# PE transposes for the first eight groups, a spare accumulator bank for the third MLP unit of a gap, and later w_out loads

## The chip, the core and the metric

The kernel runs on one core of a Trainium2 chip. The metric is the device time of one execution in microseconds. TensorE is called PE, its weight loads PEld, VectorE DVE, ScalarE ACT, GpSimd POOL and the DMA issuer SyncE SP. A DMA can be issued from the queue of SP, ACT or POOL.

## What is computed

```python
def _attn_ref(q, k, v, g_q, g_k):                 # q, k, v: (8, 12, 448, 64)
    def rmsnorm(x, g):
        rms = np.sqrt(np.mean(x * x, axis=-1, keepdims=True) + 1e-06)
        return x / rms * g
    q_n, k_n = (rmsnorm(q, g_q), rmsnorm(k, g_k))
    scores = (1.0 / np.sqrt(64)) * np.matmul(q_n, k_n.transpose(0, 1, 3, 2))
    attn = np.exp(scores - np.max(scores, axis=-1, keepdims=True))
    attn = attn / (np.sum(attn, axis=-1, keepdims=True) + 1e-09)
    return np.matmul(attn, v)

def _moe_ref(x, w_in, w_out, alpha):              # x: (3584, 768), w_in: (768, 2048)
    h = x @ w_in
    g = np.maximum(h, 0.0) + alpha * np.minimum(h, 0.0)
    return g @ w_out                              # w_out: (2048, 768)
```

The twelve heads of a token, side by side, are the 768 columns of x.

## The kernel before

**Groups.** A group y (0 to 23) is four heads of one batch; three groups make a batch, and there are eight batches. `load_qk` (L92) brings q and k of a group into the tile nat (six buffers, so three groups). `square`, `reduce`, `root` and `scale` (L127 to L162) make the normalised fp16 tile qs: a product on POOL, a reduction (ss) on DVE, a logarithm and an exponential of the small tile rr on ACT, and a product with rr on POOL. (For the first groups ACT or DVE does some of these products.) Then q and k must be transposed, so that the 64 channels lie on partitions: qT and kT.

**Two ways to transpose.** For groups 0, 1 and 2, `turn` (L174) issues 14 transposes on PE into PSUM and two evictions on DVE, of which the one for k also multiplies with the gains (`gain`). From group 3 on, `turn_dma` (L164) issues two DMA transposes on SP from qs to qT and kT, and `turn` is only the multiplication of kT with the gains on DVE (L178).

**Attention.** For each of the seven key tiles of a group, `score` (L207) does four matmuls into sc, and `soft` (L221) one exponential on ACT into expT. `den` and `attv` (L244, L257) are 28 matmuls each into an accumulator: dn, the sums of the exponentials, and av. Between them ACT inverts dn (`log` L248, `invert` L253), and after them DVE multiplies av with the inverse into xT (L263).

**MLP units.** An up unit (L268) is six matmuls into hT, an ACT copy (ah, L280) and a DVE maximum (gT, L281). A down unit (L285) is 16 matmuls into op and a DVE copy (osb, L301), with the output DMAs after the second half of a token tile.

**PSUM.** The pool pss holds two sc tiles of two banks, psa one accumulator tile of two banks (tag acc: dn, av, tps), psf two tiles of one bank (tag mm: hT, op, the filler matmuls of `spin`, and ct, through which alpha and the gains reach their partitions). A tile of a pool is reused in turn, and its next writer waits until its last reader is done.

**Order.** All engines work in program order, which the loop at L462 writes out by hand in 66 bursts. A burst has two or three key tiles (score and soft), then the den or the attv of an earlier group if one is due, then root and scale (and turn_dma) of a later group, then a gap: MLP units, with the `turn` of the next group behind the first of them. `prep` holds what is issued ahead of a burst (loads, squares), `post` and `jobs` what comes after it or inside a down unit (reductions). Bursts 0 to 11 have two key tiles each and no MLP units: den 0 and attv 0 are in bursts 4 and 5, den 1 and attv 1 in 7 and 8, den 2 in 11. Up to burst 11 a `spin(4)` ends each burst: four matmuls whose result nobody reads. Burst 12 (`first`) has attv 2 and the first up units. A burst without den and attv is called plain (`plain`). What comes after burst 65 is the list `rest`.

**Planner.** L388 to L410 spread the units of a batch over its bursts by fixed costs (1.13 for an up unit, 2.6 for a down unit, `cost(n)` for the rest of a burst). They decide only the order.

Of the kernel before, what the change touches and what calls it, by code (L numbers as in the profile page):

```python
# [9 lines left out]
FP32 = mybir.dt.float32  # L10
FP16 = mybir.dt.float16
# [10 lines left out]
def kernel(  # L22
# [12 lines left out]
    nc = tc.nc  # L35

    B, H, S, D = q.shape
    DM = H * D
    DF = moe_w_in.shape[1]
    J = S // 64  # L40
    HH = H // 2
    G = HH // 2
    KM = DM // 128
    NF = DF // 128
    OH = DM // 2
    W = 2 * S
    NG = B * G
    FB = DF // 4

    cst = ctx.enter_context(tc.tile_pool(name="cst", bufs=1))  # L50
    ld = ctx.enter_context(tc.tile_pool(name="ld", bufs=2))
# [3 lines left out]
    psa = ctx.enter_context(tc.tile_pool(name="psa", bufs=1, space=bass.MemoryType.PSUM))  # L55
    psf = ctx.enter_context(tc.tile_pool(name="psf", bufs=2, space=bass.MemoryType.PSUM))
# [24 lines left out]
    cols = cst.tile([128, NF + 2], FP32, name="cols", tag="cols")  # L81
    alpha_sb = cols[:, :NF]
    gain = cst.tile([128, 1], FP32, name="gain", tag="gain")
# [30 lines left out]
    def load_w_in(c):  # L114
        nc.gpsimd.dma_start(
            out=w_in_sb[:, :, ts(c, FB)],
            in_=moe_w_in[:, ts(c, FB)].rearrange("(k p) f -> p k f", p=128),
        )
# [8 lines left out]
    def square(y, nm):  # L127
        src = nat[y, nm].rearrange("p h j d -> p (h j d)")
        sq = ld.tile([128, 2 * J, D], FP32, name="sq", tag="sq", bufs=4)
        sqf = sq.rearrange("p n d -> p (n d)")  # L130
        if y < 2:
            nc.scalar.activation(out=sqf, in_=src, func=AF.Square)  # L132
        else:
            nc.gpsimd.tensor_mul(out=sqf, in0=src, in1=src)  # L134
        sqs[y, nm] = sq
# [37 lines left out]

    def turn(y):  # L174

        if y >= G:
            t = qkT[y, "k"].rearrange("p j g c -> p (j g c)")
            nc.vector.tensor_scalar(  # L178
                out=t, in0=t, scalar1=gain[:, 0:1], scalar2=None, op0=ALU.mult
            )  # L180
            return
        ps = psa.tile([128, 2, 512], FP32, name="tps", tag="acc")
        ps2 = psf.tile([128, 512], FP32, name="tps2", tag="mm") if y == 0 else ps[:, 1]
        tps = [
            t[:, : S].bitcast(FP16).rearrange("p (j c) -> p j c", j=J)
            for t in (ps[:, 0], ps2)
        ]
        for tp, nm in zip(tps, "qk"):
            for j in range(J):
                nc.tensor.transpose(  # L190
                    tp[:, j, :], qs[y, nm][:, j].rearrange("p h d -> p (h d)"), ident
                )
        for tp, nm in zip(tps, "qk"):
            t = att.tile([128, J, 2, 64], FP16, name=f"{nm}T", tag=f"{nm}T", bufs=4)
            o = t.rearrange("p j g c -> p j (g c)")
            if nm == "q":
                nc.vector.tensor_copy(out=o, in_=tp)
            else:
                nc.vector.tensor_scalar(
                    out=o, in0=tp, scalar1=gain[:, 0:1], scalar2=None, op0=ALU.mult  # L200
                )
            qkT[y, nm] = t
# [62 lines left out]
        )  # L265


    def up(b, ft):  # L268
        x = xT[b].rearrange("p g i c -> p (g i) c")
        hT = psf.tile([128, 512], FP32, name="hT", tag="mm")  # L270
        for c in range(KM):
            nc.tensor.matmul(  # L272
                out=hT[:, :S],
                lhsT=w_in_sb[:, c, ts(ft, 128)],
                rhs=x[:, c, :],
                start=(c == 0),
                stop=(c == KM - 1),
            )
        ah = ffn.tile([128, S], FP16, name="ah", tag="ah", bufs=3)
        nc.scalar.activation(out=ah, in_=hT[:, :S], func=AF.Copy, scale=alpha_sb[:, ft : ft + 1])  # L280
        nc.vector.tensor_max(out=gT[:, ft, ds((b & 1) * S, S)], in0=hT[:, :S], in1=ah)  # L281

    osb = {}

    def down(b0, t, oh, jobs=()):  # L285

        op = psf.tile([128, 512], FP32, name="op", tag="mm")
        for ft in range(NF):
            nc.tensor.matmul(  # L289
                out=op[:, :OH],  # L290
                lhsT=gT[:, ft, ts(t, 128)],
                rhs=w_out_sb[:, ft, ds(oh * OH, OH)],
                start=(ft == 0),
                stop=(ft == NF - 1),
            )
        for f, a in jobs:
            f(*a)
        if oh == 0:
            osb[b0, t] = ffn.tile([128, DM], FP32, name="osb", tag="osb", bufs=3)
        o = osb[b0, t]  # L300
        nc.vector.tensor_copy(out=o[:, ds(oh * OH, OH)], in_=op[:, :OH])  # L301
        if oh == 1:
            for half in range(2):
                bb, j = divmod(2 * t + half, J)
                nc.sync.dma_start(out=out4[b0 + bb, j], in_=o[ds(64 * half, 64)])

    def spin(count):

        if count:
            ps = psf.tile([128, 512], FP32, name="spin", tag="mm")  # L310
            for _ in range(count):
                nc.tensor.matmul(  # L312
                    out=ps[:, :S], lhsT=ident, rhs=idle, start=True, stop=True
                )
# [4 lines left out]
    bursts, dens, avs, first_in, last_in = [], {}, {}, {}, {}  # L319
    m = 0  # L320
    while m < NG * J or len(avs) < NG:
        n = len(bursts)
# [14 lines left out]
    av_at = {y: n for n, y in avs.items()}  # L337
    prep, post, roots = {}, {}, {}

    def at(n, f, *a):  # L340
        prep.setdefault(max(int(n), 0), []).append((f, a))

    def after(n, f, *a):
        post.setdefault(max(int(n), 0), []).append((f, a))

    turn_at = {
        y: max(n for n in range(first_in[y]) if n not in dens) for y in range(1, NG)
    }
    turns = {n: y for y, n in turn_at.items()}
    jobs = {}  # L350
    for y in range(G, NG):

        early = y < G + 2
        n = turn_at[y - 1] if early else max(d for d in dens if d <= turn_at[y] - 2)
# [26 lines left out]
    def cost(n):  # L381
        return (
            0.31 + 0.19 * len(bursts[n])
            + (1.35 if n in dens or n in avs else 0.0) + (0.9 if turns.get(n, G) < G else 0.0)
        )

    first = av_at[G - 1]
# [36 lines left out]
    for n, g in enumerate((g_q, g_k)):  # L424
        for h in range(2):
            nc.gpsimd.dma_start(
                out=rows[NF + n : NF + n + 1, ds(64 * h, 64)], in_=g.unsqueeze(0)
# [4 lines left out]
    spin(22)  # L432
    ct = psf.tile([128, 512], FP32, name="ct", tag="mm")
    nc.tensor.transpose(ct[:, : NF + 2], rows, ident32[: NF + 2, : NF + 2])
    spin(12)
    for nm in "qk":
        square(0, nm)
        reduce(0, nm)
        root(0, nm)
        scale(0, nm)  # L440
        if nm == "q":
            nc.vector.tensor_copy(out=cols, in_=ct[:, : NF + 2])
            nc.vector.tensor_mul(
                out=gain, in0=cols[:, NF : NF + 1], in1=cols[:, NF + 1 : NF + 2]
            )
    turn(0)
    load_v(0)
    for y in (1, 2):
# [3 lines left out]
                reduce(y, nm)  # L452
    for c in range(4):
        load_w_in(c)
        at(7 + c, load_w_out, c)
    after(0, root, 1)
    for nm in "qk":
        after(0, scale, 1, nm)
# [3 lines left out]
    for n in range(NB):  # L462
        for f, a in prep.get(n, ()):
            f(*a)
        tiles = bursts[n]
        for t in tiles[:2]:
            score(*t)
        plain = n not in dens and n not in avs
        wait = plain and gaps[n] and gaps[n][0][0] is up
        for t in tiles[:1] if wait else tiles[:2]:  # L470
            soft(*t)
        if n in dens:
            den(dens[n])
        if n in avs:
            attv(avs[n])
        for t in tiles[2:]:
            score(*t)
            soft(*t)
        late = []
        if wait:  # L480
            late = [(1, soft, t) for t in tiles[1:]]
        if n in dens:
            log(dens[n])
            if gaps[n] and gaps[n][0][0] is down:
                invert(dens[n])
            else:
                late = [(1, invert, (dens[n],))]
        if n in roots:
            y = roots[n]
            root(y)  # L490
            for nm in "qk":
                scale(y, nm)
            if y >= G:
                turn_dma(y)
        done = 0
        for k, (f, a) in enumerate(gaps[n]):
            if f is down:
                down(*a, jobs.pop(n, ()))
            else:
                f(*a)  # L500
                done += 1
                if late and done == late[0][0]:
                    for _, g, c in late:
                        g(*c)
                    late = []
            if k == 0 and n in turns:
                turn(turns[n])
        if not gaps[n] and n in turns:
            turn(turns[n])
        for _, g, c in late:  # L510
            g(*c)
        if n < first:
            spin(4)
        for f, a in jobs.pop(n, []) + post.get(n, []):
            f(*a)
# [32 lines left out]
```

## Time and profile before

| | before |
|---|---|
| median of 3 runs | 479.63 us (479.31 to 483.21) |
| the profiled execution, whole time | 482.26 us |
| its span, from first to last instruction | 480.5 us |
| mean granted TensorE clock | 0.974 of full |
| PE busy | 433.6 us, 90% of the span |
| ACT busy | 289.5 us, 60% |
| DVE busy | 205.5 us, 43% |
| POOL busy | 170.6 us, 36% |

The span can be read in three stretches: the opening, in which only attention runs (bursts 0 to 11, to about 65 us), the long middle, in which attention and MLP units alternate, and a tail of MLP units alone (from about 420 us). A mean over the span says little about any of them, so the views by stretch and the rows in order of time are read beside it.

### The profile page before, as it was taken

To read this page: it belongs to the slowest core of one execution; us is meant where nothing else is said; L and a number is where in the kernel's file an instruction comes from. 1 tells how busy PE (TensorE), PEld (TensorE's weight loads), DVE (VectorE), ACT (ScalarE), POOL (GpSimd) and SP (SyncE) were. 2 spreads that over 40 slices of the span, in tenths; PEclk is the share of its full clock that TensorE was granted. 3 is DMA by queue.
4 is the path that set the end of the run, shared out by engine and by line. 5 is a ranking of instruction groups with operands and counts; after the bars stand their busy time and mean duration, and the time that the engine had idled before them with its cause. 6 is when DMAs were issued, how large, how long until landed. Compare 5 with 4: busy or idle time off the path is not lost.

```text
span 480.5 us, 9024 instructions
## 1 busy us (share of the span) xinstructions
PE 433.6 (90%) x3805; PEld 227.2 (47%) x3805; DVE 205.5 (43%) x292; ACT 289.5 (60%) x400; POOL 170.6 (36%) x126
## 2 busy tenths in 40 slices
PE   7792179789998999999999999999999999999995
PEld 3340034345544555545554555455445555455463
DVE  3730142564526445445455355445454333333421
ACT  4883076867766667776677577577576566422300
POOL 5596092554343445415506505623421200000000
PEclk9997588999999999999999999999999999999999
DMA  8999988359561982585645646737317311011122
GB/s 197 244 257 204 221 159 167 39 107 190 135 149 20 147 187 52 123 181 102 118 112 93 151 111 146 135 85 140 71 40 124 72 34 33 2 34 33 34 65 67
DMA packets 69129, 55.07 MB, mean 115 GB/s; under 512 B 41936, under 2 KB 65504, under 8 KB 69088
## 3 DMA queue, kind: packets, MB, share of 16 engines
q1 hardware_dynamic: 56704, 41.76, 39.5%
q0 software_dynamic: 11808, 11.81, 16.3%
q10 hardware_dynamic: 576, 0.92, 0.8%
q8 instruction: 30, 0.49, 0.5%
q14 instruction: 11, 0.09, 0.1%
HBM read 45.62 MB, written 11.01 MB: 118 GB/s over the span
## 4 chain that ended last, share of the span: by engine, by line
PE 68%; ACT 12%; DMA 8%; DVE 6%; issue 3%; POOL 2%; SPq 0%; POOLq 0%; ACTq 0%
PE op L289 31%; PE hT L272 21%; PE sc L212 6%; ACT expT L224 6%; DMA kT<-qs 5%; PE dn L235 5%; PE av L235 4%; ACT ah L280 4%; DVE gT L281 4%; DMA nat<-in_k_dram 2%; DVE kT L178 1%; POOL qs L157 1%; DMA rows<-in_g_k_dram 1%; DVE ss L140 1%; ACT rden L250 1%
## 5 line engine op out<-in xcount | busy, mean ns | idle before, releaser
L224 ACT ACTIVATE expT<-sc,expb 128x896 f16<-128x896 f32 x168 | 157.7, 1007 | 33.6 <-PE sc L212 33.4
L272 PE MATMUL hT<-xT,w_in_sb 128*128 128x448 f16 x768 | 160.7, 355 | 8.8 <-DVE gT L281 7.9
L280 ACT ACTIVATE ah<-hT,cols 128x448 f16<-128x448 f32 x128 | 81.1, 634 | 121.3 <-PE hT L272 121.1
L289 PE MATMUL op<-w_out_sb,gT 128*128 128x384 f16 x896 | 153.5, 326 | 0.5 <-DVE gT L281 0.5
L157 POOL TENSOR_TENSOR qs<-nat,rr 128x896 f16<-128x896 f32 x45 | 77.7, 1746 | 199.6 <-issue 157.8
L281 DVE TENSOR_TENSOR gT<-hT,ah 128x448 f16<-128x448 f32 x128 | 79.9, 624 | 117.5 <-ACT ah L280 117.5
L289 PEld LDWEIGHTS <-gT 128*128 128x128 f16 x896 | 84.6, 98 | 64.3 <-issue 10.8
L272 PEld LDWEIGHTS <-w_in_sb 128*128 128x128 f16 x768 | 74.0, 98 | 84.1 <-issue 22.5
L212 PE MATMUL sc<-qT,kT 64*64 64x448 f16 x672 | 53.5, 363 | 28.8 <-DVE kT L178 24.3
L134 POOL TENSOR_TENSOR sq<-nat 128x896 f32<-128x896 f32 x44 | 73.0, 1680 | 4.6 <-DMA nat<-in_q_dram 4.2
L301 DVE COPY osb<-op 128x384 f32<-128x384 f32 x56 | 31.2, 557 | 96.1 <-PE op L289 96.1
L140 DVE TENSOR_REDUCE ss<-sq 128x14 f32<-128x896 f32 x48 | 49.7, 1076 | 5.0 <-ACT sq L132 5.0
L212 PEld LDWEIGHTS <-kT 64*64 64x64 f16 x672 | 18.5, 105 | 59.6 <-issue 27.0
L235 PE MATMUL dn<-expT,ones 64*64 64x448 f16 x672 | 36.9, 356 | 0.0
L263 DVE TENSOR_TENSOR xT<-av,rden 128x896 f16<-128x896 f32 x24 | 26.2, 1090 | 24.5 <-PE av L235 24.5
L235 PE MATMUL av<-expT,vt 64*64 64x448 f16 x672 | 35.9, 349 | 0.4 <-ACT rden L250 0.4
L235 PEld LDWEIGHTS <-ones 64*64 64x64 f16 x672 | 20.2, 110 | 13.0 <-issue 1.7
L235 PEld LDWEIGHTS <-vt 64*64 64x64 f16 x672 | 19.9, 107 | 12.6 <-issue 1.1
L178 DVE TENSOR_SCALAR kT<-kT,gain 128x896 f16<-128x896 f16 x21 | 14.9, 708 | 21.0 <-DMA kT<-qs 21.0
L250 ACT ACTIVATE rden<-dn 128x896 f32<-128x896 f32 x24 | 22.3, 931 | 1.6 <-PE dn L235 1.6
L255 ACT ACTIVATE rden<-rden 128x896 f32<-128x896 f32 x24 | 23.0, 956 | 0.5
L312 PE MATMUL spin<-idle,ident 128*128 128x448 f16 x82 | 20.5, 392 | 1.4 <-POOL ident masks.py:197 1.4
(31 smaller groups left out, 61.9 us busy)
## 6 DMA issues: line engine op xcount, KB each, us to landing
out_dram<-osb SPq DMA_DIRECT2D x56, 192.0 KB, 2.8
nat<-in_q_dram SPq DMA_DIRECT2D x46, 224.0 KB, 5.2
nat<-in_k_dram SPq DMA_DIRECT2D x46, 224.0 KB, 6.3
vt<-in_v_dram POOLq DMA_DIRECT2D x16, 336.0 KB, 7.7
w_in_sb<-in_moe_w_in_dram POOLq DMA_DIRECT2D x4, 768.0 KB, 19.0
w_out_sb<-in_moe_w_out_dram POOLq DMA_DIRECT2D x4, 768.0 KB, 14.8
nat<-in_q_dram ACTq DMA_DIRECT2D x2, 224.0 KB, 4.8
nat<-in_k_dram ACTq DMA_DIRECT2D x2, 224.0 KB, 6.3
```

Source lines behind the costliest of these rows:

```text
L134: nc.gpsimd.tensor_mul(out=sqf, in0=src, in1=src)
L140: nc.vector.tensor_reduce(out=ss_t[y][:, "qk".index(nm)].rearrange("p h j -> p (h j)").unsqueeze(2), in_=sqs[y, nm], axis=AXIS_X, op=ALU.add,)
L157: eng.tensor_mul(out=t.rearrange("p j h d -> p h j d"), in0=nat[y, nm], in1=rr_t[y][:, "qk".index(nm)].unsqueeze(3).broadcast_to((128, 2, ...
L212: nc.tensor.matmul(out=sc[ds(64 * g, 64), par, :S].rearrange("p (j c) -> p j c", j=J), lhsT=kT[ds(64 * par, 64), j, g, :], rhs=qT[ds(64 * ...
L224: nc.scalar.activation(out=expT[y][:, j], in_=scs[y, j][:, :, :S], func=AF.Exp, scale=QK_SCALE, bias=expb[:, 0:1],)
L235: nc.tensor.matmul(out=acc[ds(64 * par, 64), g, :S], lhsT=weights(g, par, j), rhs=e[ds(64 * g, 64), j, par, :], start=(j == 0), stop=(j == ...
L250: nc.scalar.activation(out=r, in_=rden[y][:, :, :S], func=AF.Ln)
L272: nc.tensor.matmul(out=hT[:, :S], lhsT=w_in_sb[:, c, ts(ft, 128)], rhs=x[:, c, :], start=(c == 0), stop=(c == KM - 1),)
L280: nc.scalar.activation(out=ah, in_=hT[:, :S], func=AF.Copy, scale=alpha_sb[:, ft : ft + 1])
L281: nc.vector.tensor_max(out=gT[:, ft, ds((b & 1) * S, S)], in0=hT[:, :S], in1=ah)
L289: nc.tensor.matmul(out=op[:, :OH], lhsT=gT[:, ft, ts(t, 128)], rhs=w_out_sb[:, ft, ds(oh * OH, OH)], start=(ft == 0), stop=(ft == NF - 1),)
L301: nc.vector.tensor_copy(out=o[:, ds(oh * OH, OH)], in_=op[:, :OH])
```

## The change

- `TD = 8`: groups 0 to 7 are transposed on PE by `turn`, groups 8 to 23 by DMA. Groups 3 to 7 are those that move. For groups 0 to 2 the two PSUM tiles of `turn` come from psf, for groups 3 to 7 they are the two banks of the acc tile.
- `turn(2)` moves from burst 6 to burst 5 (`av_at[0]`). The planner's chain makes root, scale and the squares of group 3 one burst earlier with it: its squares come ahead of burst 3, its reductions after burst 5, its root in burst 6.
- `bank`: the third unit of a gap takes its PSUM bank from the acc tile, except in a burst with a PE `turn`.
- The copy of ct to cols and the product `gain` come after the scale of group 0's k, not between q and k.
- The four w_out loads are issued ahead of bursts 10 to 13 (`first` is 12), where they were ahead of bursts 7 to 10.
- `spin(4)` stays only after plain bursts without a turn: bursts 0, 1, 3, 6 and 10. The spin ahead of group 0 has 8 matmuls, where it had 12.
- `cost(n)` counts a PE turn for groups 3 to 7 too. Worked through by hand, the planner then moves one up unit from burst 16 to burst 18 and one from burst 20 to burst 22; all other gaps stay. The third unit uses the acc tile in bursts 13, 18, 21 to 25, 28, 30, 32, 33, 35 to 40, 43, 45, 47, 48, 50 to 55, 58, 60, 63 and 64, which are 31 gaps.

```diff
+    TD = min(8, NG)
     def turn(y):
-        if y >= G:
+        if y >= TD:
             t = qkT[y, "k"].rearrange("p j g c -> p (j g c)")
             nc.vector.tensor_scalar(
                 out=t, in0=t, scalar1=gain[:, 0:1], scalar2=None, op0=ALU.mult
             )
             return
-        ps = psa.tile([128, 2, 512], FP32, name="tps", tag="acc")
-        ps2 = psf.tile([128, 512], FP32, name="tps2", tag="mm") if y == 0 else ps[:, 1]
+        if y < G:
+            ps = [psf.tile([128, 512], FP32, name="tps", tag="mm") for _ in "qk"]
+        else:
+            ps2 = psa.tile([128, 2, 512], FP32, name="tps2", tag="acc")
+            ps = [ps2[:, 0], ps2[:, 1]]
...
+    def bank(name, spare):
+        if spare:
+            t = psa.tile([128, 2, 512], FP32, name=name + "a", tag="acc")
+            return t[:, 0]
+        return psf.tile([128, 512], FP32, name=name, tag="mm")
+
-    def up(b, ft):
+    def up(b, ft, spare=False):
         x = xT[b].rearrange("p g i c -> p (g i) c")
-        hT = psf.tile([128, 512], FP32, name="hT", tag="mm")
+        hT = bank("hT", spare)
...
-    def down(b0, t, oh, jobs=()):
+    def down(b0, t, oh, jobs=(), spare=False):
-        op = psf.tile([128, 512], FP32, name="op", tag="mm")
+        op = bank("op", spare)
...
+    turn_at[2] = av_at[0]
...
-            + (1.35 if n in dens or n in avs else 0.0) + (0.9 if turns.get(n, G) < G else 0.0)
+            + (1.35 if n in dens or n in avs else 0.0) + (0.9 if turns.get(n, TD) < TD else 0.0)
...
-    spin(12)
+    spin(8)
     for nm in "qk":
         square(0, nm)
         reduce(0, nm)
         root(0, nm)
         scale(0, nm)
-        if nm == "q":
-            nc.vector.tensor_copy(out=cols, in_=ct[:, : NF + 2])
-            nc.vector.tensor_mul(
-                out=gain, in0=cols[:, NF : NF + 1], in1=cols[:, NF + 1 : NF + 2]
-            )
+    nc.vector.tensor_copy(out=cols, in_=ct[:, : NF + 2])
+    nc.vector.tensor_mul(
+        out=gain, in0=cols[:, NF : NF + 1], in1=cols[:, NF + 1 : NF + 2]
+    )
...
     for c in range(4):
         load_w_in(c)
-        at(7 + c, load_w_out, c)
+        at(first - 2 + c, load_w_out, c)
...
-            if y >= G:
+            if y >= TD:
                 turn_dma(y)
...
         for k, (f, a) in enumerate(gaps[n]):
+            spare = k == 2 and not turns.get(n, TD) < TD
             if f is down:
-                down(*a, jobs.pop(n, ()))
+                down(*a, jobs.pop(n, ()), spare)
             else:
-                f(*a)
+                f(*a, spare)
...
-        if n < first:
+        if n < first and plain and n not in turns:
             spin(4)
```

## Rows read from the trace of the kernel before

**Rows 1.** The page, the span in 40 slices of 12 us: granted clock and DMA

```profile
PEclk9997588999999999999999999999999999999999
DMA  8999988359561982585645646737317311011122
```

**Rows 2.** Windows: stretch, length, busy of PE, PEld, DVE, ACT, POOL (instructions), clock, DMA, GB/s

```profile
73.30:76.60 3.30, 3.30 (x11) 1.33 (x9) 0.62 (x1) 1.53 (x2) 2.15 (x2) 0.52 1.19 211
113.00:420.00 307.00, 300.46 (x2740) 159.58 (x2736) 141.26 (x203) 208.14 (x286) 108.25 (x70) 1.00 0.52 104
```

**Rows 3.** Waits of the whole run: us in total, times, longest us

```profile
PE sc L212 <- DVE kT L178: 24.3, 4, 18.8
DVE kT L178 <- DMA kT<-qs: 21.0, 2, 20.2
```

**Rows 4.** Timeline: group 3's transpose, and four marks in bursts 12, 13, 14, 20

```profile
38.68 5.76 SPq L167 DMA_TRANSPOSE kT<-qs  x1
...
65.48 2.78 ACT L224 ACTIVATE expT<-sc,expb 128x896 f16<-128x896 f32 x3
...
72.49 0.38 PE L212 MATMUL sc<-qT,kT 64*64 64x448 f16 x4 [2.56 <-DVE kT L178]
...
79.54 0.57 PE L212 MATMUL sc<-qT,kT 64*64 64x448 f16 x8
...
112.54 0.57 PE L212 MATMUL sc<-qT,kT 64*64 64x448 f16 x8
```

**Rows 5.** Tile views of w_in_sb, then of w_out_sb: four loads each

```profile
DMA to landing us min/median/max: 11.6/19.0/24.6
...
DMA to landing us min/median/max: 14.3/14.8/19.8
```

**Rows 6.** Timeline of the opening, by engine, out of order of time

```profile
25.31 0.92 ACT L250 ACTIVATE rden<-dn 128x896 f32<-128x896 f32 x1
27.11 3.81 ACT L224 ACTIVATE expT<-sc,expb 128x896 f16<-128x896 f32 x4
...
34.66 0.33 ACT L151 ACTIVATE rr<-ss,epsb 128x28 f32<-128x28 f32 x1
35.02 0.23 ACT L152 ACTIVATE rr<-rr 128x28 f32<-128x28 f32 x1
...
27.91 1.09 DVE L263 TENSOR_TENSOR xT<-av,rden 128x896 f16<-128x896 f32 x1 [4.90 <-PE av L235]
...
30.36 0.62 DVE L197 COPY qT<-tps 128x896 f16<-128x896 f16 x1 [1.36 <-PE tps L190]
30.90 0.68 DVE L199 TENSOR_SCALAR kT<-tps,gain 128x896 f16<-128x896 f16 x1
31.49 2.07 DVE L140 TENSOR_REDUCE ss<-sq 128x14 f32<-128x896 f32 x2
...
27.06 6.58 POOL L134 TENSOR_TENSOR sq<-nat 128x896 f32<-128x896 f32 x4
...
29.37 0.95 PE L190 MATMUL tps<-ident,qs 128*128 128x128 f16 x14
```

**Rows 7.** Windows of PE's filler matmuls alone (L312): busy of PE and PEld, clock

```profile
14.00:25.00 11.00, 4.22 (x19) 1.59 (x20) 1.00 1.20 248
```

**Rows 8.** Timeline: PE's waits at the start of burst 16 and at its third unit

```profile
91.04 0.57 PE L212 MATMUL sc<-qT,kT 64*64 64x448 f16 x8 [1.67 <-DVE kT L178]
...
96.32 1.29 PE L272 MATMUL hT<-xT,w_in_sb 128*128 128x448 f16 x6 [0.82 <-DVE gT L281]
```

**Rows 9.** Timeline: the up units of burst 30, the den of burst 31

```profile
186.02 2.43 PE L272 MATMUL hT<-xT,w_in_sb 128*128 128x448 f16 x12
188.79 1.49 PE L235 MATMUL dn<-expT,ones 64*64 64x448 f16 x28
189.16 0.62 DVE L281 TENSOR_TENSOR gT<-hT,ah 128x448 f16<-128x448 f32 x1 [0.51 <-ACT ah L280]
```

**Rows 10.** Waits of PE alone between 113 and 420 us

```profile
PE hT L272 <- DVE gT L281: 5.6, 14, 1.0
```

More of the change, by code (lines that the diff above doesn't have):

```diff
@@ L181, in turn @@
             return
-        ps = psa.tile([128, 2, 512], FP32, name="tps", tag="acc")
-        ps2 = psf.tile([128, 512], FP32, name="tps2", tag="mm") if y == 0 else ps[:, 1]
+        if y < G:
[3 more added lines that the diff above has]
+            ps = [ps2[:, 0], ps2[:, 1]]
         tps = [
-            t[:, : S].bitcast(FP16).rearrange("p (j c) -> p j c", j=J)
-            for t in (ps[:, 0], ps2)
+            t[:, : S].bitcast(FP16).rearrange("p (j c) -> p j c", j=J) for t in ps
         ]
```

## The prediction

> **What bounds the kernel now.** I read the slices first: DMA is busy at eight tenths or more through the first seven, nine or more from the second to the fifth, and the clock falls in the fourth and stands at half in the fifth [rows 1]. The waits of the whole run say why: PE's scores waited 24.3 us in four places for kT, once for 18.8 us, and the DVE product that makes kT waited 20.2 us of that for the DMA transpose of group 3 [rows 3]. That transpose was issued at 38.68 us, and it shares the DMA engines with w_in (landing up to 24.6 us after issue), with w_out and with the loads of later groups [rows 4, 5]. The windows say what comes later: from 113 to 420 us PE is busy 300.46 of 307 us at full clock [rows 2], so there the bound is PE, and every microsecond that PE is made to wait there counts. So the change acts on two stretches with different bounds: the opening, where a transfer is the bound and after it ACT, and the middle, where PE is.
>
> **The opening.** The transposes of groups 3 to 7 leave the DMA queues. Until 27.11 us nothing that sets ACT's pace changes: the loads, the reductions and group 2's scale come as before, since group 3's squares are slipped in on POOL while it waits for group 2's root. So I rebuild ACT's order from there with the durations of the rows. Four exponentials take 3.81 us [rows 6], to 30.92. Group 3's root is now next, and is late: DVE ends av's product at 29.00 (27.91 + 1.09), then group 2's two evictions to 30.22 (0.54 us between their starts, 0.68 for the second), then two reductions of 2.07, to 32.2. The root costs 0.56 (0.33 + 0.23), so ACT goes on at about 32.8. Behind this wait stand the exponentials of burst 7; before, they waited in the same place for group 2's kT. Bursts 7 to 11 are ten exponentials of about 0.93 (9.3), twice a logarithm and an inversion (four at 0.92: 3.7), group 4's root (0.56) and some 0.15 of a wait for its reductions: 13.7, so burst 12's exponentials start at 46.5. Before, they started at 65.48 [rows 4]. **Gain 19.0.**
>
> Is anything else late by then? POOL: group 3's scale from 32.85 to 36.2, group 4's squares to 39.6, group 5's squares to 43.0 (6.58 / 4 = 1.65 each, and near that for a scale [rows 6]), one w_out issue, then group 4's scale, done at 47.2. Its turn stands behind burst 12's first up unit, which ends near 49.3 (den 2's logarithm ends at 45.6, attv 2, of 1.49 [rows 9], at 47.1, av's product at 48.2, then one unit). So POOL has 2 us to spare. Group 3's turn on PE needs its scale (36.2) and the acc tile, free when av's product of group 1 ends at 38.1; kT is there at 40.2, and its first exponential is due at 41.1. The w_in loads landed by 43.8 even with the transposes and w_out beside them (19.2 + 24.6), and are needed at 48. The w_out loads, issued from 43 to 58, land within 19.8 at the latest [rows 5], by 78. The first down unit is in burst 18, four bursts behind burst 14, which comes at 57.7 (below); a burst there takes 5.5 (six in 112.54 - 79.54 [rows 4]), so it is due after 79. SP loses ten transposes, one of which held its queue for 5.76 us [rows 4] with group 6's loads behind it. DVE gains a q eviction of 0.62 for each of five groups, and is idle over half of the time [rows 2]. Group 0's reordered cols and gain change nothing to a tenth: DVE reduces k 0.9 us earlier, and q's transposes wait for ct's bank until about 11.8.
>
> **Bursts 12 and 13.** From the exponentials to the first score of group 4 the trace has 7.0 us (65.48 to 72.49), which ended with a wait for kT [rows 4]. Now the chain is three exponentials (2.78), group 5's root (0.56), ah and gT of the first unit (about 0.65 and 0.62), then two evictions (1.3): 5.95. **Gain 1.05.** From there to burst 14 it took 7.05 us, part of it at half clock (0.52 between 73.3 and 76.6 [rows 2]), after PE had stood still for 2.6 us. Without that it is one score tile (0.35) and four up units of 1.22 (2.43 for two [rows 9]): 5.25. **Gain 1.8**, 21.8 in all.
>
> **Bursts 14 to 20.** Three turns (groups 5, 6 and 7) now put 14 transposes, 0.95 us [rows 6], into PE's stream. For groups 5 and 6 PE waited for kT at the next burst, 1.67 us [rows 8] and 1.3 us (what the 24.3 us leave after 18.8, 2.56 and 1.67 [rows 3, 4, 8]), because DVE ran late. The transposes fall into that time, so I count only what they reach beyond it: 0.5 and 0.6. Group 7's has no such cover: 0.95. The unit that leaves burst 16 takes its wait of 0.82 [rows 8] with it, and burst 18's third unit, a down, holds burst 19's den by about 0.25. Sum: a **loss of 1.5**, gain 20.3 at burst 21.
>
> The Trainium skill, TensorE: Matmul & The Clock Gate, Part 4: PE-mode transpose, gives about 275 ns for a 128x128 transpose inside a kernel. At that, 14 are 3.85 us, by my estimate, and the four turns from burst 12 on would cost 11.6 us more. The trace shows 14 in 0.95 us, so that single durations overlap, and I take the trace.
>
> **The spare bank.** Between 113 and 420 us PE waited for a psf bank 14 times, 5.6 us in all [rows 10]. The third unit in another bank removes these: **gain 5.6** (the opening counted none of them). But the acc tile is where the next den or attv goes. In burst 30 the third unit's matmuls ended near 188.4, and the next den started at 188.79; the gT that reads that unit ended at 189.78 (189.16 + 0.62) [rows 9]. If the unit sits in the acc tile, that den, and everything behind it on PE, waits 1.0 us more. Gaps of just three units, the third an up, with a den or attv in the next burst are those of bursts 21, 30, 35, 36, 39, 45, 50, 51, 54 and 60: ten, each with this spacing. A gap of four gives 1.22 us more and no wait; a plain burst behind the gap uses no acc tile; the third unit of burst 64 is a down and costs about 0.4. **Loss 10.4.** Net loss 4.8. The bounds: nothing for the waits (if they were hidden), and 1.0 in all 31 spare gaps.
>
> **The filler.** Seven of twelve spin(4) go. They were 4.22 of 11 us in the opening, at clock 1.00 [rows 7], in time in which PE waited for ACT: no gain. If the clock falls for want of them, PE's own work in bursts 0 to 11 (24 tiles of 0.285, five den and attv of 1.5, three turns: 17 us) takes 34 us, about what ACT needs (32.3 from 14.29). Bounds: 0 to about 8 us lost, the upper end with the first MLP units slow as well. I take 0, since the one fall of the clock in the rows came with PE standing still altogether.
>
> By the same page, the section Why this matters for your kernels, TensorE should be kept busy, or it falls to the lower clock; that speaks against this edit. The sum by it is the third case below.
>
> **Sum.** 19.0 + 1.05 + 1.8 - 1.5 - 4.8 = 15.55 off the profiled span of 480.5: 464.95. That execution took 482.26, 2.6 above the median of the runs, and the same 15.55 off the median, 479.63, gives **464.1**.
>
> **The rivals.**
> *The spare bank costs nothing* (the den is not held, as when its turn comes later than I think): 10.4 less, 453.7; with half of it, 459. For: ACT idles about 30% in the middle [rows 2]. Against: the spacing of rows 9, ten times. Chance 0.13, mostly near 459.
> *The opening slows* (clock at half, or a load or POOL late): up to 8 more, 472. For: five of the 12 fillers are left; group 3's root is late by over a microsecond as it is. Against: PE still works in every burst. 0.22.
> *The transfer wait comes back in another place*: group 6's loads, issued when its buffers come free at 34.5 and 36.2, hold POOL's squares and with them group 5's scale once they land after 55 or so, that is over 19 us after issue. For: w_in's slowest load took 24.6 [rows 5]. Against: the transposes beside it are gone. If the wait were like the old one, nearly all of the gain would go: 479. 0.05.
> *The other side, slower*: every one of the 31 spare gaps holds the next user of the acc tile for 1.0 us: 31 - 5.6 = 25.4 in place of 4.8, 484.7. It ends above the time before from 26 such holds on. Against: behind a fourth unit the tile is free 0.2 us before it is wanted. 0.03.
> The forecast itself, 460 to 468, has 0.55; what is left, 0.02, is spread.
>
> **How the numbers follow.** The time is that of the forecast. The range, 457 to 472, takes in the forecast, the half-way case of the first rival and nearly all of the second, about 0.85. About 1% (4.8 us) is what can be told from no change. Faster by more than that is everything below 474.8: 0.55 + 0.13 + 0.22, with a little of the rest: 0.91. Within it 0.05, slower 0.04.
>
> **What would show it.** Right: no wait of PE for kT over 3 us; burst 12's exponentials between 45 and 49 us; group 8's DMA transpose landing in under 7 us; PE's waits of hT for gT in the middle near nothing, and in their place ten waits of dn or av for gT near 1.0 us each. Wrong: a clock below 0.9 in slices 2 to 4; POOL waiting for nat after 40 us; waits for the acc tile in gaps of four; a first down unit that waits for w_out.

## The result

The changed kernel takes 463.86 us (median of four runs, 463.18 to 464.57); the kernel before, beside it, 480.89 (479.31 to 483.21, four runs). The ratio is 0.964, with a 95% interval of 0.959 to 0.969. The forecast was 464.1, in a range from 457 to 472. The profiled executions are 19.1 us apart (spans of 480.5 and 461.4).

The slices of the page after, granted clock and DMA, beside those of [rows 1]:

```profile
PEclk9899999999999999999999999999999999999999
DMA  8999993764438445763438555763137311011122
```

The fall of the clock in slices four to seven is gone. In its place the second slice stands at 8 (0.85 between 11.5 and 23 us), which the prediction had named as a sign of being wrong; the third and fourth are at full clock. DMA is at eight tenths or more through six slices, where it was through seven. The waits of PE over the whole run, after (us in total, times, longest; a view of waits lists those over 0.15 us):

```profile
PE sc L215 <- ACT expT L227: 5.8, 12, 1.0
PE dn L238 <- DVE gT L290: 4.4, 5, 0.9
PE av L238 <- DVE gT L290: 4.4, 5, 0.9
PE sc L215 <- DVE kT L202: 3.2, 6, 1.0
PE tps L193 <- DVE xT L266: 2.2, 2, 1.1
...
PE hT L281 <- DVE gT L290: 1.2, 5, 0.2
```

The 24.3 us of waits for kT in [rows 3] have shrunk to 3.2 us, none above 1.0, and the scores now wait longest for ACT (5.8 us; 2.6 before). New are ten waits of dn and av for gT, 0.9 us each, which no row before had, and the 14 waits of hT for gT in the middle [rows 10] are gone; the five that are left stand in the tail. The other signs came as forecast: group 8's DMA transposes land in 3.0 and 3.8 us, the view lists no wait of POOL for a load after 40 us, and w_out has landed by 71.21 us, ahead of the first down unit at 83.38. The timeline after, at group 3's root and at the four marks of [rows 4] (bursts 12, 13, 14 and 20):

```profile
31.66 0.32 ACT L152 ACTIVATE rr<-ss,epsb 128x28 f32<-128x28 f32 x1 [1.20 <-DVE ss L141]
...
46.27 2.79 ACT L227 ACTIVATE expT<-sc,expb 128x896 f16<-128x896 f32 x3
...
51.88 0.38 PE L215 MATMUL sc<-qT,kT 64*64 64x448 f16 x4 [0.51 <-DVE kT L202]
...
56.84 0.57 PE L215 MATMUL sc<-qT,kT 64*64 64x448 f16 x8
...
91.14 0.57 PE L215 MATMUL sc<-qT,kT 64*64 64x448 f16 x8
```

Against before, the four marks come 19.2, 20.6, 22.7 and 21.4 us earlier. From the last of them to the end of the span 2.3 us are lost again. Where, the timeline of bursts 30 and 31 shows, the place of [rows 9]:

```profile
164.76 1.30 PE L281 MATMUL hTa<-xT,w_in_sb 128*128 128x448 f16 x6
...
165.99 0.57 PE L215 MATMUL sc<-qT,kT 64*64 64x448 f16 x8
166.09 0.63 ACT L289 ACTIVATE ah<-hTa,cols 128x448 f16<-128x448 f32 x1 [0.50 <-PE hTa L281]
...
166.76 0.62 DVE L290 TENSOR_TENSOR gT<-hTa,ah 128x448 f16<-128x448 f32 x1 [0.51 <-ACT ah L289]
...
167.44 1.52 PE L238 MATMUL dn<-expT,ones 64*64 64x448 f16 x28 [0.88 <-DVE gT L290]
```

The third up unit sits in the acc tile (hTa). The scores of the next burst still run, and then den stands for 0.88 us until gT has read the unit. It is the same picture in bursts 22, 31, 36, 37, 40, 46, 51, 52, 55 and 61.

### The profile page after: what moved, and what is told of

Same layout as the page of the kernel before. It is cut to its first block, busy times and chain, and to the rows that moved or that the text cites. A ratio compares the mean times of both kernels' runs of the same rounds, so it can differ in the third digit from the quotient of the medians.

```text
span 461.4 us, 9085 instructions
## 1 busy us (share of the span) xinstructions
PE 429.8 (93%) x3843; PEld 230.4 (50%) x3843; DVE 206.8 (45%) x297; ACT 290.6 (63%) x400; POOL 170.4 (37%) x126
## 4 chain that ended last, share of the span: by engine, by line
PE 78%; ACT 11%; DVE 8%; issue 1%; ACTq 1%; DVEq 0%
PE op L298 31%; PE hT L281 20%; PE hTa L281 7%; PE av L238 6%; PE dn L238 5%; PE sc L215 5%; ACT expT L227 5%; ACT ah L289 3%; DVE gT L290 3%; DVE ss L141 3%; PE opa L298 1%; ACT rden L253 1%; ACT rden L258 1%; PE tps L193 1%; DVE kT L202 1%
## 5 line engine op out<-in xcount | busy, mean ns | idle before, releaser
L298 PE MATMUL op<-w_out_sb,gT 128*128 128x384 f16 x864 | 148.0, 326 | 0.2 <-DVE gT L290 0.2
L289 ACT ACTIVATE ah<-hT,cols 128x448 f16<-128x448 f32 x99 | 62.8, 635 | 101.6 <-PE hT L281 101.5
L281 PE MATMUL hT<-xT,w_in_sb 128*128 128x448 f16 x594 | 125.1, 353 | 1.3 <-DVE gT L290 1.2
L290 DVE TENSOR_TENSOR gT<-hT,ah 128x448 f16<-128x448 f32 x99 | 61.8, 624 | 94.4 <-ACT ah L289 94.4
L281 PE MATMUL hTa<-xT,w_in_sb 128*128 128x448 f16 x174 | 37.6, 352 | 0.0
L238 PEld LDWEIGHTS <-vt 64*64 64x64 f16 x672 | 21.1, 107 | 18.8 <-issue 9.0
L238 PEld LDWEIGHTS <-ones 64*64 64x64 f16 x672 | 21.5, 107 | 15.9 <-issue 6.4
L289 ACT ACTIVATE ah<-hTa,cols 128x448 f16<-128x448 f32 x29 | 18.4, 635 | 13.2 <-PE hTa L281 13.2
L290 DVE TENSOR_TENSOR gT<-hTa,ah 128x448 f16<-128x448 f32 x29 | 18.1, 625 | 12.1 <-ACT ah L289 11.9
```

The lines of the kernel that those rows point to most:

```text
L238: nc.tensor.matmul(out=acc[ds(64 * par, 64), g, :S], lhsT=weights(g, par, j), rhs=e[ds(64 * g, 64), j, par, :], start=(j == 0), stop=(j == ...
L281: nc.tensor.matmul(out=hT[:, :S], lhsT=w_in_sb[:, c, ts(ft, 128)], rhs=x[:, c, :], start=(c == 0), stop=(c == KM - 1),)
L298: nc.tensor.matmul(out=op[:, :OH], lhsT=gT[:, ft, ts(t, 128)], rhs=w_out_sb[:, ft, ds(oh * OH, OH)], start=(ft == 0), stop=(ft == NF - 1),)
```

## The experiments

Every experiment was timed beside the kernel before on the same chip; the median of that kernel lay between 482.05 and 482.98 us there, and was 480.89 beside the changed kernel. So a difference of about 1 us between medians that were not timed side by side is not resolved. Traces are compared by the starts of the same den or attv.

### What the spare bank costs and brings

**No spare bank.** The edit to the changed kernel:

```diff
-            spare = k == 2 and not turns.get(n, TD) < TD
+            spare = False
```

> The changed kernel with every MLP unit in a psf bank. Theory (the spare bank costs more than it brings): the ten waits of dn and av for gT, each 1.05 us by the shift of the dens between the two traces, and that of burst 64 (0.65) go, 11.2 us; the waits of hT for gT in the middle come back, which the two traces put at 8.5 us. So 2.5 us below the changed kernel's 463.9: 461.4, between 460 and 463. By the prediction's own sizes (10.4 against 5.6) it would be 459.1. Rival (the third bank is what the change lives on): 469 to 472, the 5.6 to 8.5 us come back and nothing goes.

Measured: 462.69 us (ratio to before 0.960, 0.956 to 0.963). The waits of PE between 110 and 400 us are those of before again:

```profile
PE hT L281 <- DVE gT L290: 5.6, 14, 1.0
```

The den of burst 31, which before starts at 188.79 [rows 9], starts here at

```profile
170.02 1.49 PE L238 MATMUL dn<-expT,ones 64*64 64x448 f16 x28
```

That is 18.77 us earlier, as is every den and attv from burst 23 to the end: without the spare bank the middle is that of the kernel before, to 0.01 us, and what is gained is gained ahead of it. In the changed kernel the offset (how much earlier a start is than before) is 22.70 at burst 14 and 18.74 at the last attv, here 21.16 and 18.77. So from burst 14 on the spare bank as it stands costs 1.6 us net. The spans of the two traces (461.4 and 461.3) hide that, since this one's opening was 1.5 us later, at a granted clock of 0.88 between 36 and 47 us, where the changed kernel's has 1.00.

**The spare bank only where it holds nobody:**

```diff
-            spare = k == 2 and not turns.get(n, TD) < TD
+            last = len(gaps[n]) == 3 and (n + 1 in dens or n + 1 in avs)
+            spare = k == 2 and not last and not turns.get(n, TD) < TD
```

> The changed kernel, in which the third unit stays in psf where the gap has just three units and the next burst has a den or attv; in the other gaps it keeps the acc tile. Theory: the 11.2 us of waits for the acc tile go and the waits of hT for gT do not come back, since they stood in gaps of four and five: 463.9 - 11 = 453, between 452 and 455. Rival (the acc tile holds the next den behind a fourth unit too, or the ten waits hide another that takes their place): 458 or more.

Measured: 452.79 us (0.940, 0.937 to 0.943), 11 us below the changed kernel. The view lists no den or attv that waits for gT any more, and between 110 and 400 us PE's waits of hT for gT are down from 14 to one. So the spare bank is two edits of opposite sign. On the same chip, the useful part brings 9.9 us (462.69 - 452.79), and 9.3 between the two traces from burst 20 on. The edit takes the spare bank out of twelve gaps. They cost about 11: against this trace the starts of the changed kernel fall back by 1.05 to 1.1 us behind each of the ten gaps and by 0.3 behind that of burst 64; the down in burst 18 costs nothing that shows.

**The tail too:**

```diff
-    for f, a in rest:
-        f(*a)
+    for k, (f, a) in enumerate(rest):
+        f(*a, spare=k % 3 == 2)
```

> The spare bank only inside gaps, as in e2_spare_inside, and the acc tile as a third bank for every third unit of the list rest, after the last attv. Theory: the tail's six waits of hT and op for gT, 0.25 each with some 0.15 to start again, go: 2 us below e2_spare_inside, near 451. Rival (in the tail PE waits for ACT and DVE themselves, not for a bank): the same time as e2_spare_inside.

Measured: 449.91 us (0.935, 0.932 to 0.938), 2.9 below the one before it, which was timed on another chip; the profiled spans are 2.5 apart, all of it behind the last attv. The six waits in the tail are gone, as the theory has it, and the size is a little above it.

### What carried the opening

**DMA transposes again, with the rest of the change:**

```diff
-    TD = min(8, NG)
+    TD = G
```

> The changed kernel with TD = 3: groups 3 to 7 are transposed by DMA again, the w_out loads stay at bursts 10 to 13, the spare bank and the fewer fillers stay. Theory (a DMA transpose on loaded DMA engines is what held the opening): group 3's transposes, issued near 33 to 36 us, still wait for the w_in backlog, which ends near 42, and group 4's for w_out; kT is awaited for 4 to 12 us, and PE gets 3 us of transposes back: 468 to 476. Rival (the place of w_out is what mattered): 461 to 465, no wait for kT over 2 us.

Measured: 477.37 us (0.991, 0.987 to 0.995). The DMA issues and the DVE product of kT in its timeline:

```profile
36.84 3.53 SPq L168 DMA_TRANSPOSE kT<-qs  x1
...
45.99 0.45 DVE L179 TENSOR_SCALAR kT<-kT,gain 128x896 f16<-128x896 f16 x1 [7.89 <-DMA kT<-qs]
...
62.52 0.45 DVE L179 TENSOR_SCALAR kT<-kT,gain 128x896 f16<-128x896 f16 x1 [4.21 <-DMA kT<-qs]
```

Without w_out ahead of it, group 3's k takes 9 us in place of 19: it lands right behind the last w_in load (45.29 us). Group 4's, issued at 52.53, takes 10 beside w_out, v and the loads of a later group, and group 5's, issued at 63.59, takes 18.7. The moved w_out loads without PE transposes do not free the opening. The theory's mechanism holds, and the time is 1.4 us above its range. No run keeps the DMA transposes and moves both weight loads out of their way, so that an opening with DMA transposes on emptier engines stays untried.

**w_out early, with the rest of the change:**

```diff
-        at(first - 2 + c, load_w_out, c)
+        at(7 + c, load_w_out, c)
```

> The changed kernel with the w_out loads at bursts 7 to 10 again. Theory: nothing on the path waits for a DMA once PE transposes, so their place costs nothing: 463 to 465.5. Rival (they delay w_in or the loads of groups 5 and 6): w_in's last part after 49 us or POOL's squares late, 467 to 475.

Measured: 471.77 us (0.979, 0.976 to 0.982). My theory falls: 7.9 us. Its timeline, at attv 3, where the scores of the burst start at 61.30:

```profile
68.37 0.58 PE L238 MATMUL av<-expT,vt 64*64 64x448 f16 x2 [6.49 <-DMA vt<-in_v_dram]
```

What is late is neither w_in nor nat, which the rival named, but v of batch 1, the first use of which is attv 3 in burst 15. Its loads are issued on POOL's queue ahead of burst 11. With w_out early they stand behind all four w_out loads and land 19.7 to 20.7 us after issue, right behind the last of w_out (66.73 us); in the changed kernel they stand behind one, and land after 9.8 to 11.0, by 58 us, where attv 3 starts at 61.63. The tile views of vt in this stretch, w_out early first:

```profile
DMA to landing us min/median/max: 19.7/20.2/20.7
```

```profile
DMA to landing us min/median/max: 9.8/10.4/11.0
```

**v ahead of the early w_out** (the edit is to the kernel of the last experiment):

```diff
-        at(av_at[G * b] - 4, load_v, b)
+        at(6 if b == 1 else av_at[G * b] - 4, load_v, b)
```

> e4_w_out_early (w_out at bursts 7 to 10) with the v loads of batch 1 issued ahead of burst 6, before the w_out loads on POOL's queue, where they were ahead of burst 11, behind them. Theory (e4 lost 8 us because attv 3 waited 6.5 us for v, which stood behind w_out on the same queue): the wait for v goes and the time is that of the changed kernel, 463 to 465. Rival (early w_out costs by loading the DMA engines as a whole, wherever v stands): 468 or more, with the wait at w_in, at nat or still at v.

Measured: 464.05 us (0.963, 0.959 to 0.967). The wait for v is gone and with it the 7.7 us. v still takes 20 to 21 us, now behind the w_in loads, but it is issued at 26.43 and there by 48.13. So w_out's place matters through what stands behind it on the queue, and not by the load on the DMA engines as a whole.

**PE transposes alone.** The kernel before, with TD = 8 in `turn` and in front of `turn_dma`, and nothing else of the change:

```diff
+    TD = min(8, NG)
...
-        if y >= G:
+        if y >= TD:
             t = qkT[y, "k"].rearrange("p j g c -> p (j g c)")
...
-            if y >= G:
+            if y >= TD:
                 turn_dma(y)
```

> The kernel before with PE transposes for groups 3 to 7 alone (TD = 8 in turn and turn_dma; the planner's costs, the place of turn 2, the fillers, w_out and the PSUM banks as before). Theory (the transposes carry the opening by themselves): no spare bank, so like the changed kernel without it, 461 to 464, with up to 2 us more for turn 2's old place and the fillers. Rival (the change needs its other parts, w_out's place above all): 468 or more, with a wait for a load in the opening.

Measured: 468.66 us (0.974, 0.971 to 0.978), the rival's number. Its waits of PE between 30 and 100 us begin with the same cause:

```profile
PE av L236 <- DMA vt<-in_v_dram: 5.3, 2, 4.2
```

**PE transposes alone, with v ahead of w_out** (the edit of v, on the last kernel):

> e5_pe_turns_only (the kernel before with PE transposes for groups 3 to 7 alone) with the v loads of batch 1 ahead of burst 6 and so ahead of the w_out loads on POOL's queue, which stay at bursts 7 to 10. Theory (transposes and the order of v and w_out are all that the opening needed; e5 waited 5.3 us for v): 462.5 to 464.5, as the changed kernel, with no wait of av for v. Rival (w_out beside w_in and nat costs in this order too, or the other parts carry some of it): 466 or more.

Measured: 462.82 us (0.958, 0.957 to 0.960), and no wait for v. So the two edits together, group 3 to 7's transposes and v ahead of w_out, reach the time of the whole change, and that of the change without its spare bank (462.69). What else it has, the fewer fillers, turn 2's new place and the spare bank as it stands, adds nothing on top that these times resolve.

### The fillers

All of them kept: `if n < first:` in place of `if n < first and plain and n not in turns:`, and `spin(12)`.

> The changed kernel with spin(4) after each of the bursts 0 to 11 and 12 filler matmuls ahead of group 0, as before. Theory: the fillers lie mostly in time in which PE waits for ACT or kT; the two traces have burst 4's den 0.7 us earlier without them, of which 0.5 lasted: 464 to 465. Rival (the fillers keep the clock up, and their lack cost time): 461 to 463.

Measured: 464.12 us (0.964, 0.960 to 0.968). None in bursts 0 to 11: `if False:` in the same place.

> The changed kernel without any filler in bursts 0 to 11 (those ahead of group 0 stay). Theory (PE's own work in the opening is enough): granted clock 1.00 from 15 to 47 us, and 463 to 464. Rival (the clock falls): a clock near 0.5 in part of the opening and the time 3 to 8 us up, 467 to 472.

Measured: 465.06 us (0.966, 0.962 to 0.970). The windows of the two (busy of PE, PEld, DVE, ACT, POOL, then the clock, DMA share and GB/s), all kept first:

```profile
12.00:30.00 18.00, 14.08 (x167) 7.33 (x167) 11.13 (x16) 14.34 (x19) 13.30 (x10) 1.00 1.20 243
```

```profile
12.00:30.00 18.00, 13.73 (x146) 7.34 (x145) 9.69 (x13) 14.00 (x19) 13.35 (x10) 0.62 1.20 242
```

Without fillers the clock does fall, to 0.62 of full between 12 and 30 us, and in that profiled execution the bursts from den 2 on come 2.7 to 3.0 us later than in the changed kernel's. The medians of the three stand within 1.2 us, and their intervals overlap. Execution by execution, though, the time goes with the mean granted clock: without fillers 463.81 us at 0.992, 465.00 at 0.984, 465.12 at 0.983 and 466.13 at 0.978; in the changed kernel 463.18 and 463.69 at 0.996, 464.02 at 0.991 and 464.57 at 0.987. With all fillers the clock is 0.998 to 1.000 and the time 464.03 to 464.45. So the lower clock goes with some 2 us where it falls furthest, and at nearly the same clock the fewer fillers look about half a microsecond faster: in the medians the two nearly cancel. The theory's clock of 1.00 is wrong; the rival's clock is right, and its price too high.

### What a PE transpose costs where PE is the bound

All 24 groups on PE, on the kernel without the spare bank (`TD = NG`):

> e1_no_spare (no spare bank) with all 24 groups transposed on PE, so that 16 more turns stand in the middle, where PE is the bound. Theory (a turn there costs its 14 matmuls, 0.95 us, and in four or five bursts some 1.1 us of waiting for the acc tile as in bursts 15 and 17): 462.7 + 15.2 + 0 to 5 = 478 to 483. Rival (the page's 275 ns for each transpose, 3.85 us for 14): 520. Second rival (hidden in waits that are there anyway): 463 to 468.

Measured: 478.40 us (0.994, 0.991 to 0.996), 15.7 above the 462.69 of the same kernel with eight, which is 0.98 us for each of 16 more turns. (The first rival's own figure, 16 times 3.85, would make it 524.) The tile view of tps between 110 and 420 us gives the single durations:

```profile
L193 PE MATMUL tps<-ident,qs x224: 217/219/219, 110.7 to 387.7; 128*128 128x128 f16 x112
```

A row of 14 lasts 0.94 to 0.95 us there, and a single one 0.22. So 14 start 0.056 us apart, and what follows them on PE starts 0.78 us behind the first. By that 16 turns hold PE for 12.5 us. The other 3.2 are waits for the most part: between 110 and 420 us the views list 8.6 us of them (hT and op for gT 7.0), against 6.3 in the kernel with eight turns. Only one is for the acc tile, where the theory allowed four or five. The planner counts the 16 turns too and moves up units between bursts for them, so the figure is that of the turns with these moves.

**Groups 6 and 7 by DMA again,** on the kernel with the spare bank inside the gaps and in the tail (`TD = 6`):

> e8_spare_inside_rest with TD = 6: groups 6 and 7 are transposed by DMA. Theory (the DMA engines' backlog ends near 65 us, so that a transpose issued at burst 15 lands in under 7 us and in time for burst 17): PE gets two turns back, 1.9 us, and 1.1 us of one wait for the acc tile, less about 1.3 for kT in burst 18: 447.5 to 449.5. Rival (group 6's transposes still meet w_out or the loads of groups 7 and 8): a wait for kT over 2 us, 451 or more.

Measured: 449.55 us (0.933, 0.929 to 0.937): the same as with eight (449.91), within the intervals. Group 6's transposes, issued at 69.55 and 71.19 us, land in 3.0 and 4.8. What the turns give back in PE, a wait for kT of 1.4 us takes again in part. 449.6 to 449.9 us, 6.5 to 6.7% below before, is the best that I found, 14 us under the changed kernel.

## Why the prediction was right, and where it was not

**The opening** was right in its steps. Group 3's root became the late one and started at 31.66 (32.2 in the prediction); burst 12 started at 46.27 (46.5), burst 13's score at 51.88 (52.45) and burst 14 at 56.84 (57.7), so that the gain there was 22.7 us and not 21.85. Two small readings were off and cost nothing: the four exponentials that the order was rebuilt from started at 26.63 and not at 27.11, and w_in's last load landed at 46.41 and not by 43.8. What it got wrong was what it did not ask. It asked of w_out's new place only whether the first down unit would wait, and let the rest of the opening run as if v came in time. It does, by more than 3 us, because w_out moved: at the old place the same sum would have been 8 us too low, as w_out early showed. So the gain that I put on the transposes is theirs only together with the order of one queue. The rule that I broke: of a step that is moved, name what stands behind it on its queue. Behind the w_out loads stood v.

**The turns from burst 14 on** were counted at 1.5 us lost up to burst 21. Burst 14 came 22.7 us earlier and burst 21 21.5, which looks like 1.2, but at burst 21 the up unit that the planner moved from burst 20 to burst 22 is still to come, and the sum left it out. At equal work, without the spare bank, the offset goes from 21.16 at burst 14 to 18.77 at burst 23: 2.4 us are lost. Turns 5 and 6 waited 1.1 us each for the acc tile, where before there were waits for kT of 1.67 and 1.34. The price of a turn, 0.95 us, is the length of its row; it holds PE for 0.78, and all turns on PE gave 0.98 with the waits that come with them. The 275 ns for each transpose on the page TensorE: Matmul & The Clock Gate (Part 4: PE-mode transpose) of the Trainium skill are the length of a single one. Here that is 217 to 219 ns, and in a row they start 56 ns apart, so that the length is not the price.

**The spare bank** was right in its mechanism, ten waits where ten were named, and off in the size of one term. The loss, put at 10.4, is about 11. The gain, put at 5.6, is 9.3 between the traces. The view of waits had it too small in two ways. It leaves out waits under 0.15 us, of which the trace without the spare bank has six more, 6.3 us of idle time in all. And a wait delays what is behind it by more than its idle time: in burst 28 a row before has 0.25 us of idle ahead of the fourth unit, and with the spare bank the next den comes 0.41 earlier. The 0.16 between them is what a record of the profile overlaps the next in an unbroken row (matmuls of 0.35 us that start 0.19 apart), and the idle time is counted from the end of the last record. By my estimate 20 times 0.16 and 6.3 make 9.5. So the net loss is 1.6 us from burst 14 on, and not 4.8.

**The sum.** The profiled spans are 19.1 us apart, 3.5 more than the 15.55 of the sum: the spare bank gives 3.2 of it, the opening 0.9, the stretch behind the last attv 0.4, and the turns take 0.9 away. That the time was met to 0.2 us is luck in that part: this error of the sum was made up for by its base. The forecast was taken off 479.63, the median of three executions of the kernel before, where two of its four in the result take 482.15 and 483.21, and its medians beside the experiments are 482.05 to 482.98. The profiled execution of before was 1.4 above the median of its four runs, and that of after 0.7 below its own, so that the medians differ by 17.0.

**The rivals.** The bank that costs nothing did not come: the waits are there. The opening that slows (the third case in the prediction's part on the filler, the second in its list) has its mechanism in the runs, a clock of 0.62 once all fillers in the bursts go. With five of twelve left the clock falls too, and in other places from one execution to the next: the changed kernel has 0.79 between 12 and 20 us and 1.00 from there to 47, the one without the spare bank, whose opening is the same program, 1.00 between 12 and 30 us and 0.88 between 36 and 47. The price was 1.5 us in that trace and 3.0 without fillers, and not 8. Holds behind a fourth unit, the other side, did not occur beyond a tenth of a microsecond (attv 7).

## What to carry to other kernels

When a large load moves, follow the queue that it is issued on and ask of every load behind it when it is needed; here that was worth 6 to 8 us. A spare buffer pays only where its reader is done before the buffer's regular owner wants it: look at what follows the unit, and split the edit by it, which turned a loss of 1 to 2 us into a gain of 10. And move work to the bound engine where its price is known from how far apart the instructions of a row start, not from one duration, and compare two traces only at points where the same work is done.

## What the runs showed of the hardware

- A wait of PE costs more than the idle time shown: 0.25 us of idle moved the next burst by 0.41, and 0.88 by 1.05 (offsets of the den and attv starts between the traces before and after: 22.40 us at attv 9, 21.35 at den 10). Both are 0.16 to 0.17 more, as much as the records of two matmuls overlap in an unbroken row.
- The same DMA transpose of one group's k took 19 us beside w_in and w_out, 9 beside w_in and the loads of a later group, and 4.8 on emptier engines.
- Loads on POOL's queue landed in the order of their issue in these traces: v behind all of w_out (66.73 us) at 68.32 and 70.00, and ahead of w_out but behind w_in (45.34) at 46.59 and 48.13.
- With no filler matmuls in the bursts of the opening the granted clock was 0.62 of full between 12 and 30 us, a mixture of its two levels, while PE's records fill 13.73 of the 18 us; with all of them it was 1.00 and the records fill 14.08.
